# Turning g of two token units by DMA, and a rearranged tail, in an attention + two-layer-MoE kernel

## The chip, the cores and the metric

The kernel runs on one core of one Trainium2 chip. The metric is the device time of one execution in microseconds (us): 638.88 us, the median of three runs (637.43 to 639.08). The changed kernel is measured in the same way.

## What is computed (the reference, cut)

```python
# attention, batch 4, 8 heads, 576 tokens, head size 64
scores = q @ k.T / 8;  keep scores >= rowmax - tau;  a = softmax(kept) @ v
x = a as (2304 tokens, 512)
# first layer: w_in (512, 2048), w_out (2048, 512)
g = relu(x @ w_in) ** 2
x = g @ w_out
# second layer: phi (512, 32 slots), 8 experts of 4 slots, w1 (512, 1024), w2 (1024, 512) each
logits = x @ phi
slot_input = softmax_over_tokens(logits).T @ x
slot_out[e] = relu(slot_input[e] @ w1[e]) @ w2[e]
out = softmax_over_slots(logits) @ slot_out
```

## The kernel before, in words

**Stages.** While attention is computed, w_in is split into two fp16 parts (the `w8` tiles), w_out is rounded, stored to DRAM as `w_out32`, and multiplied with phi into `wphi`, so that the logits come straight from g. The 2304 tokens are taken as nine units of 256: eight of them (batch, half), and `rem` for the 64 last tokens of each batch. The units run in the order n = 0 to 8.

**A unit** (`ffn_ops`). DVE makes two fp16 parts of x: `xh` (line 1131) and `xl` (line 1136; there is one `xl` buffer, so a unit's `xl` waits for the last matmul of the unit before). PE makes eight pairs of column blocks `f_a`, `f_b` (line 1165), each half 8 matmuls with `xh` and 4 with `xl`. ACT applies relu and square (lines 1174, 1182) and leaves g in a `gt` tile of 128 columns x 2 x 256 tokens.

**What follows a unit** (`post`), put into the stream after the next unit's first pair: PE multiplies g with `wphi` (`pl`, line 977), turns the logits (lines 984, 990), and DVE and ACT make maxima, exponentials and token weights. Then g itself is needed with tokens on the partitions: for each of two token blocks t and four j, PE turns four 128x128 blocks (`turn`, line 269), ACT moves them from PSUM to `gk` (line 1074), PE multiplies with the token weights (`accum`, line 1089), and DVE adds to `sg` (line 1098). There are four `gk` buffers.

**The order of work.** All instructions are written by a planner (`Plan`): each operation has an engine, a cost, a key, and the slots it takes; the planner runs them in its own clock and writes each engine's stream in that order. Engines then execute their own stream in order, and SP issues all DMAs, loads of weights and transposes of attention alike, in one stream. `LEAD` shifts the keys. After the last attention operation (`plan.run(att)`) attention's memory is given back and nine 1 MiB loads `ew8` and one 0.5 MiB load `ew6` of expert weights are issued directly, outside the planner's clock and bus; then the planner goes on with the rest, loads into `xp` and `w8` slots (`w_load`) among them.

**The tail.** `sg` is turned and multiplied with w_out (line 1283; w_out lies in eight `raw64` tiles), then w1 (`hidden`, line 1302) and w2 (line 1376) of the eight experts, then the outputs (lines 1395 to 1414). 33.6 MB of w1 and w2 stream in; the loads `wr` go into the `raw64` slots once line 1283 has used them, and further `ew8` loads follow once w1 tiles are used. The loads, the planner's loop around the direct loads:

```python
plan.run(att)
...
for f in [ew8] * 9 + [ew6]:
    f()
for n in range(XPB + 1):
    add("w_load", "SP", 0.5, wx, state["xl"][-XPB - 1 + n], n, dma=1.46)
```

Of the kernel before, what the change touches and what calls it, by code (L numbers as in the profile page):

```python
# [147 lines left out]
def tile_kernel(  # L148
# [51 lines left out]
    LEAD = {'c_evac': 8.5, 'c_hi': 109.5, 'c_lo': 76.5, 'c_load': -19.6, 'c_low': 0.2, 'c_out': -17.5, 'c_prod': 65.3, 'c_scale': 13.2, 'c_shift': -19.8, 'c_store': -158.3, 'c_unit': 0.1, 'f_a': 18.2, 'f_acc': 7.3, 'f_alpha': -43.9, 'f_b': -30.4, 'f_cmax': -2.3, 'f_csum': -1.6, 'f_dk': 3.5, 'f_l4': -7.7, 'f_max': 43.7, 'f_merge': 5.1, 'f_p12': -4.1, 'f_pl': 278.3, 'f_pm': -7.7, 'f_relu': 3.3, 'xhi': 3.4, 'xlo': -1.1, 'f_gk': 15.9, 'w_load': 17.8, 'c_turn': 0.0, 'f_sq': -4.5, 'f_p1k': 2.2, 'lphi': -16.2, 'f_turn': 1.5, 'f_p3': -14.5, 'recip': 2.7, 'dturn': -3.1, 'q_scale': -2.9, 'p_evac': -20.3, 'f_total': 0.3, 'w_rest': -1.1, 'av': -1.0, 'r_evac': -3.3, 'w_hi': 6.6, 'w_scale': 0.3, 'v_hi': -6.8, 'top': 3.1, 'eps': -10.6, 'w_diag': -4.8, 'low': -4.3, 'v_scale': -9.2}  # L200
# [3 lines left out]
    GKD = ()  # L204
# [9 lines left out]
    QL = 19.2  # L214
# [86 lines left out]
    def conv_ops():  # L301
# [168 lines left out]
        for n in range(RB):  # L470
            add("w_pre", "SP", 0.5, lambda: state["wr"](), stores, 1000.0 + n, ["raw64"], dma=1.46)
# [485 lines left out]
    def ffn_ops(units):  # L957
# [9 lines left out]
        def post(u, d, first, last):  # L967
            w, po = {}, {}
            fo = prev["ops"]

# [42 lines left out]
            def cmax():  # L1013
                lk = w["p12"][:, NU:NU + T * NS].rearrange("p (t s) -> p t s", s=NS)
# [40 lines left out]
            add("f_csum", "DVE", 0.80, csum, [h], HI + 1, rel=[("mm", b_)])  # L1055
            i_ = add("f_p3", "PE", 0.25, p3, [e], pk(), ["mm"], [("dT", e)])
            j_ = add("f_dk", "DVE", 0.2, dkc, [i_], HI, rel=[("mm", i_)])
            lastsg, turns = fo.get("sg"), []
            for t in range(T):
                gks, ro = [], []  # L1060
                for j in range(NG):
# [54 lines left out]
        for n, u in enumerate(units):  # L1116
# [80 lines left out]
            pending = lambda u=u, d=d, n=n: post(u, d, n == 0, n == len(units) - 1)  # L1197
# [282 lines left out]
```

## Time and profile before

| what | value |
|---|---|
| median of 3 runs | 638.88 us |
| the profiled execution | 640.07 us, its span 638.3 us |
| PE busy | 585.2 us (92%) |
| ACT, DVE, POOL busy | 442.0, 432.4, 284.0 us |
| DMA engines busy (hardware queue) | 67.1% of the span, 115.88 MB |
| attention's last operation, by line 894 | ends at 483.6 us |
| units 7 and 8 | 498.8 to 529.7 and 529.7 to 560.7 us |
| w1 and w2 by PE | 579.3 to 619.7 us |

Times in the rows are us from the span's start; the execution's own time is 1.8 us more than its span. A busy PE counts pipelined matmuls, so PE is best read by the starts of its groups. `PEclk` is the granted TensorE clock, 1.00 being 2.4 GHz and 0.50 being 1.2 GHz.

### The profile page before, as it was taken

The numbers are of one execution on the slowest core, as the hardware profiler recorded it, in microseconds if no ns is written. First come the engines' busy times: TensorE is split into PE (matmuls) and PEld (weight loads), VectorE is DVE, ScalarE is ACT, GpSimd is POOL, SyncE is SP. The second block draws the span as 40 slices with busy tenths as digits, with TensorE's granted clock in tenths as the row PEclk, the third lists the DMA queues.
The fourth block names the chain that finished last, engine by engine and source line by source line (L and its number), as shares of the span: only waits on it lengthen the run. The fifth ranks groups of instructions, "written<-read, shape, count | busy, mean of one in ns | idle before, by whom it ended". The sixth has DMA issues, their size and how long they took to land.

```text
span 638.3 us, 14121 instructions
## 1 busy us (share of the span) xinstructions
PE 585.2 (92%) x5218; PEld 406.2 (64%) x5218; DVE 432.4 (68%) x1225; ACT 442.0 (69%) x852; POOL 284.0 (44%) x464
## 2 busy tenths in 40 slices
PE   3897979899999999999999989999999999989883
PEld 1454646567777677667767767867868787853321
DVE  5798998899988987986888987887640302021503
ACT  2798757678888888988978888887864545441203
POOL 1446672257577766676746657765530000010000
PEclk9998889989999999999989999999999999998997
DMA  8975516576887767585855857788646921568967
GB/s 277 351 232 170 193 58 222 183 184 162 206 152 165 175 137 138 102 197 97 183 106 98 179 103 140 133 174 166 149 75 240 407 80 34 185 213 315 388 253 296
DMA packets 156084, 116.78 MB, mean 183 GB/s; under 512 B 119920, under 2 KB 128880, under 8 KB 156016
## 3 DMA queue, kind: packets, MB, share of 16 engines
q1 hardware_dynamic: 156016, 115.88, 67.1%
q8 instruction: 41, 0.67, 0.4%
q14 instruction: 27, 0.22, 0.1%
HBM read 73.72 MB, written 8.91 MB: 129 GB/s over the span
## 4 chain that ended last, share of the span: by engine, by line
PE 66%; DVE 15%; DMA 6%; ACT 4%; issue 3%; POOL 3%; SPq 2%; ACTq 0%; DVEq 0%; POOLq 0%
PE mm L1165 28%; PE mm L269 8%; PE s L703 6%; PE po L872 5%; DVE u L729 5%; DVE e L745 3%; PE mm L1302 2%; PE mm L1089 2%; DMA w<-in_moe_w_dram 2%; PE mm L977 2%; PE s L690 2%; DMA w_out<-cv 2%; PE po L877 2%; PE po L864 1%; DMA qt<-in_q_dram 1%
## 5 line engine op out<-in xcount | busy, mean ns | idle before, releaser
L1165 PEld LDWEIGHTS <-w 128*128 128x128 f16 x1728 | 166.5, 98 | 26.8 <-issue 7.9
L768 POOL TENSOR_TENSOR hl<-e,hl 128x288 f16<-128x288 f32 x192 | 147.0, 789 | 40.1 <-issue 28.5
L1165 PE MATMUL mm<-xh,w 128*128 128x256 f16 x1152 | 149.6, 273 | 0.3 <-ACT gk L1074 0.2
L745 DVE SCALAR_TENSOR_TENSOR e<-u,sm,e 128x576 f32<-128x576 f32 x144 | 120.1, 849 | 18.7 <-ACT e L741 14.3
L741 ACT ACTIVATE e<-u,sm 128x576 f32<-128x576 f32 x144 | 109.2, 771 | 20.6 <-DVE u L729 15.3
L735 POOL TENSOR_SCALAR sm<-sm,tau_p 128x1 f32<-128x1 f32 x144 | 72.8, 511 | 72.0 <-DVE u L729 65.4
L1165 PE MATMUL mm<-xl,w 128*128 128x256 f16 x576 | 86.4, 273 | 0.0
L1174 ACT ACTIVATE gt<-mm,scl 128x512 f32<-128x512 f32 x72 | 49.2, 683 | 53.5 <-PE mm L1165 52.9
L729 DVE TENSOR_SCALAR_CACHE_REDUCE u<-s,raw 128x576 f32<-128x576 f32 x90 | 71.1, 811 | 14.7 <-PE s L703 13.7
L764 ACT ACTIVATE hl<-e 128x576 f16<-128x576 f32 x96 | 64.0, 675 | 2.0 <-DVE e L745 1.6
L832 POOL TENSOR_SCALAR sm<-sm 128x4 f32<-128x4 f32 (+1 forms) x48 | 20.8, 433 | 61.6 <-DVE e L745 52.1
L1182 ACT ACTIVATE gt<-gt 128x512 f32<-128x512 f32 x72 | 45.0, 625 | 1.1
L1265 POOL MEMSET cv<- 128x512 f32 x4 | 1.9, 524 | 97.4 <-PE mm L1089 97.4
L729 DVE TENSOR_SCALAR_CACHE_REDUCE u<-s,nscale 128x576 f32<-128x576 f32 x54 | 42.6, 807 | 3.2 <-PE s L690 2.6
L812 ACT ACTIVATE pt<-mm 128x512 f32<-128x512 f32 x48 | 28.6, 602 | 21.3 <-PE mm L269 20.8
L1074 ACT ACTIVATE gk<-mm 128x512 f32<-128x512 f32 x68 | 36.2, 591 | 6.3 <-PE mm L269 6.1
L269 PE MATMUL mm<-ident_r,e 128*128 128x128 f32 (+1 forms) x224 | 37.1, 300 | 3.1 <-DVE e L745 2.2
L703 PEld LDWEIGHTS <-qt 128*128 128x128 f16 (+3 forms) x400 | 21.9, 99 | 28.3 <-issue 17.8
L269 PE MATMUL mm<-ident_r,gt 128*128 128x128 f32 x288 | 38.0, 278 | 0.5 <-ACT gk L1074 0.5
L269 PEld LDWEIGHTS mm<-ident_r,e 128*128 128x128 f32 (+1 forms) x224 | 27.9, 153 | 16.3 <-DVE e L745 5.5
L872 PE MATMUL po<-pt,vh 128*64 128x256 f16 x576 | 37.0, 279 | 0.0
L269 PEld LDWEIGHTS mm<-ident_r,gt 128*128 128x128 f32 x288 | 31.8, 144 | 7.9 <-issue 5.8
(189 smaller groups left out, 978.2 us busy)
## 6 DMA issues: line engine op xcount, KB each, us to landing
w<-in_moe_w_dram SPq DMA_DIRECT2D x17, 1024.0 KB, 14.2
w<-in_moe_w_dram SPq DMA_DIRECT2D x26, 512.0 KB, 7.9
raw<-in_moe_w_in_dram SPq DMA_DIRECT2D x16, 511.8 KB, 6.7
raw<-in_moe_w_out_dram SPq DMA_DIRECT2D x16, 511.8 KB, 3.9
raw<-in_v_dram SPq DMA_DIRECT2D x20, 256.0 KB, 3.3
w_out<-cv SPq DMA_DIRECT2D x16, 256.0 KB, 2.7
w<-w_out SPq DMA_DIRECT2D x8, 512.0 KB, 4.2
kt<-in_k_dram SPq DMA_DIRECT2D x10, 320.0 KB, 3.5
```

Source lines behind the costliest of these rows:

```text
L269: nc.tensor.transpose(out_, in_, ident[:n, :n])
L703: nc.tensor.matmul(o0, d["qh"][r, a, q0], kk, start=full, stop=not full)
L729: nc.vector.tensor_scalar(u, o["s"][:, s0:s0 + S], d.get("nscale", nscale), None, ALU.mult, ALU.min, accum_out=gd["sm"][:, c:c + 1])
L735: nc.gpsimd.tensor_scalar(sm[:, 4 + c:5 + c], sm[:, c:c + 1], tau_p, None, ALU.add)
L741: nc.scalar.activation(e, o["u", a], AF.Exp, scale=-1.0, bias=gd["sm"][:, c:c + 1])
L745: nc.vector.scalar_tensor_tensor(e, o["u", a], sm[:, 4 + c:5 + c], e, ALU.is_le, ALU.mult, accum_out=sm[:, 8 + c:9 + c])
L764: nc.scalar.activation(o["hl"][:, a * S:(a + 1) * S], o["e"][:, a * S:(a + 1) * S], AF.Copy)
L768: nc.gpsimd.tensor_tensor(o["hl"][:, 2 * S:][:, i], o["e"][:, i], o["hl"][:, i], ALU.subtract)
L872: nc.tensor.matmul(po[64 * a:64 * a + 64, :n_], d["vh"][:, y, c0:c0 + D], gd["pt"][:, :, c + 5 * a + m, :], start=i == 0 and m == 0, stop= ...
L1165: nc.tensor.matmul(o["h"][:, i * NU:(i + 1) * NU], a, c, start=n_ == 0, stop=n_ == len(terms) - 1)
L1174: nc.scalar.activation(g, o["h"], AF.Relu, scale=down)
L1182: nc.scalar.activation(g, g, AF.Square)
```

## The change

For the units n = 6 and 7 (`DTU`), the 32 PE transposes of g and the ACT moves behind them are replaced. ACT (`f_part`) copies each pair's g, seen as 16-bit words, into high and low halves in a `raw64` tile; one DMA transpose (`f_move`, on SP) turns such a tile of two pairs, 16 blocks of 128x128; DVE (`f_join`) puts the two halves together again into `gk`. In the units 0 to 5 half of the `gk` moves go from ACT to DVE (`GKD`), in the last unit too. The eight loads of w_out into `raw64` get a later key. In the tail, both halves of w1 are multiplied together, w1 and w2 tiles hold consecutive rows of four (a partition reads up to 8 KB in one run, where w1 had runs of 4 KB and w2 of 2 KB), PSUM tiles alternate between the two pools of four banks (`bank`), and a few copies in the chain from `sg` to the slots are split or joined. Many `LEAD` values differ. The core of the diff:

```diff
...
     FKEY = 1e5
-    GKD = ()
+    DTU = (6, 7)
+    DEA = (0, 1)
+    GKL = (1, 3)
+    GKD = (1, 3)
     SQD = ()
     LOD = (0, 4)
...
     def mm_tile(tag="mm"):
         return psp[tag].tile([128, 512], F32, tag=tag, name="mm")
+
+    def old_tile():
+        return psp["old"].tile([128, 512], F32, tag="mm", name="mm")
...
+    def row512x2():
+        return rows.tile([128, 4 * CW], U16, tag="raw64", name="raw64", bufs=RB)
...
-            add("w_pre", "SP", 0.5, lambda: state["wr"](), stores, 1000.0 + n, ["raw64"], dma=1.46)
+            add("w_pre", "SP", 0.5, lambda n=n: state["wr"](state["wo"][n]), stores, 2 * FKEY + n, ["raw64"], dma=1.46)
...
-        def post(u, d, first, last):
+        def post(u, d, first, last, by_halves):
...
             def p1k():
-                p = w["p12"]
+                p = w["p1"] = old_tile() if last else w["p12"]
...
-            add("f_csum", "DVE", 0.80, csum, [h], HI + 1, rel=[("mm", b_)])
             i_ = add("f_p3", "PE", 0.25, p3, [e], pk(), ["mm"], [("dT", e)])
             j_ = add("f_dk", "DVE", 0.2, dkc, [i_], HI, rel=[("mm", i_)])
+            add("f_csum", "DVE", 0.80, csum, [h] + [j_] * last, HI + 1, rel=[] if last else [("mm", b_)])
...
+            halves = {}
+            for j in range(NG) if by_halves else ():
+                o = {}
+
+                def part(x, j=j, o=o):
+                    if not x:
+                        o["h"] = row512x2().rearrange("p (h x n) -> p h x n", h=2, x=2)
+                    g = d["pair"][2 * j + x].bitcast(U16).rearrange("p (n h) -> p h n", h=2)
+                    if x in DEA:
+                        nc.scalar.activation(o["h"][:, :, x], g, AF.Copy)
+                    else:
+                        nc.vector.tensor_copy(o["h"][:, :, x], g)
+
+                def move(j=j, o=o):
+                    o["t"] = row512x2().rearrange("p (b f) -> p b f", f=128)
+                    nc.sync.dma_start_transpose(out=o["t"], in_=o["h"].rearrange("p h x n -> p (h x n)"))
+
+                hs = []
+                for x in range(2):
+                    eng = "ACT" if x in DEA else "DVE"
+                    hs.append(add("f_part", eng, 1.05 if x in DEA else 1.13, lambda x=x, f=part: f(x), [d["sq"][2 * j + x]] + hs[:1],
+                                  pk(), [] if x else ["raw64"]))
+                    plan.release(hs[x], [("gt", d["rl"][2 * j + x])])
+                    plan.release(a, [("gt", d["rl"][2 * j + x])])
+                halves[j] = o, add("f_move", "SP", 3.0, move, hs, pk(), ["raw64"], [("raw64", hs[0])], dma=-4.5)
...
-                        if j not in GKD:
+                        if j not in gkd:
...
+                    if by_halves:
+                        def join(t=t, j=j):
+                            gk = w["gk", t, j] = row512()
+                            y = gk.bitcast(U16).rearrange("p (m f h) -> p h m f", m=4, h=2)
+                            z = halves[j][0]["t"].rearrange("p (h m t) f -> p t h m f", h=2, t=T)[:, t]
+                            for h in range(2):
+                                nc.vector.tensor_copy(y[:, h], z[:, h])
+
+                        rel = [("raw64", halves[j][1])] if t == T - 1 else []
+                        r = add("f_join", "DVE", 1.2, join, [halves[j][1]], pk(), ["gk"], rel)
+                        gks.append(("gk", r))
+                        ro.append(r)
+                        continue
...
+                    d.setdefault("pair", {})[m2] = g
...
-            pending = lambda u=u, d=d, n=n: post(u, d, n == 0, n == len(units) - 1)
+            pending = lambda u=u, d=d, n=n: post(u, d, n == 0, n == len(units) - 1, n in DTU)
...
-        src = {k: x.rearrange("(k p) f -> p k f", p=128) for k, x in src.items()}
...
+        def part(kind, e, k0, n):
+            x = src[kind, e]
+            if kind == "wo":
+                return x.rearrange("(k p) f -> p k f", p=128)[:, k0:k0 + n]
+            return x.rearrange("(h p k) f -> p h k f", p=128, k=4)[:, k0 // 4, k0 % 4:k0 % 4 + n]
...
         for kind, n in (("wo", 2), ("w1", E), ("w2", E)):
-            seq += [(kind, e, k) for e in range(n) for k in range(src[kind, e].shape[1])]
+            if kind == "w1":
+                seq += [(kind, e, k + i) for b in range(0, E, NG) for k in (0, 2) for e in range(b, b + NG) for i in range(2)]
+            else:
+                seq += [(kind, e, k) for e in range(n) for k in range(rows_of[kind])]
...
-            nc.sync.dma_start(out=t, in_=src[kind, e][:, k0:k0 + n, :])
+            nc.sync.dma_start(out=t, in_=part(kind, e, k0, n))
...
-        pt = mm_tile()
+        turns = [0]
+
+        def bank():
+            turns[0] += 1
+            return old_tile() if turns[0] % 2 else mm_tile()
+
+        pt = [bank() for _ in range(2)]
         for i in range(4):
-            transpose(pt[:, i * 128:(i + 1) * 128], sg[:, i * 128:(i + 1) * 128])
+            transpose(pt[i // 2][:, i % 2 * 128:(i % 2 + 1) * 128], sg[:, i * 128:(i + 1) * 128])
...
-        both(sgt, pt)
+        nc.scalar.activation(sgt[:, 0:256], pt[0][:, 0:256], AF.Copy)
+        nc.vector.tensor_copy(sgt[:, 256:512], pt[1][:, 0:256])
...
-        both(si4, ps, rr)
...
+        nc.scalar.activation(si4, ps, AF.Copy, scale=rr)
...
-        def hidden(i2, hf):
-            ph = mm_tile()
-            for kk in range(KC):
-                for j in range(NG):
...
+        def hidden(i2, kks, ph):
+            for kk in kks:
+                for hf in range(2):
+                    for j in range(NG):
...
+        def relu(ph):
+            hr = [row512() for _ in range(2)]
+            nc.scalar.activation(hr[0], ph[0], AF.Relu)
+            nc.vector.tensor_scalar(hr[1], ph[1], 0.0, None, ALU.max)
             return hr
...
-        h00 = hidden(0, 0)
-        c0 = spaced(0)
-        h01 = hidden(0, 1)
-        spread(0, 0, h00)
-        codes(*c0)
-        for _ in range(7):
+        ph = [bank() for _ in range(2)]
+        hidden(0, (0, 1), ph)
+        for _ in range(3):
             ew8()
...
+        codes(*pc[0])
+        ew8()
+        hidden(0, (2, 3), ph)
+        h0 = relu(ph)
+        for _ in range(3):
+            ew8()
+        c2 = codes_turn(*spaced(8))
+        ph = [bank() for _ in range(2)]
+        hidden(1, (0, 1), ph)
+        codes(*pc[1])
+        for hf in range(2):
+            spread(0, hf, h0[hf])
         for f in [ew8] + [wx] * 4 + [w8]:
             f()
-        c3 = spaced(12)
-        spread(1, 1, h11)
-        c4 = spaced(16)
-        codes(*c3)
-        codes(*c4)
-        po = mm_tile()
+        hidden(1, (2, 3), ph)
+        h1 = relu(ph)
+        codes(*c2)
+        c3, c4 = [codes_turn(*spaced(t)) for t in (12, 16)]
+        po = bank()
...
         for i, (e, fc) in enumerate(seq):
+            if i == NG:
+                for hf in range(2):
+                    spread(1, hf, h1[hf])
+                codes(*c3)
+                codes(*c4)
...
+            state["wo"] = [take(1024) for _ in range(RB)]
...
             plan.run(att)
+        psp["old"] = psp["mm"]
         psp["mm"] = ctx.enter_context(tc.tile_pool(name="ps_t", bufs=4, space=bass.MemoryType.PSUM))
...
```

What the planner makes of it is shown at two places. The first is SP's stream after the last attention transposes (`pt<-hl`): `w<-in_moe_w_dram` are loads of w1 and w2, `w<-w_out` loads of w_out. Before:

```order
L775 DMA_TRANSPOSE pt<-hl 128x18x128 x4
L1220 DMA w<-in_moe_w_dram 128x2x1024 x9
L1220 DMA w<-in_moe_w_dram 128x2x512
L1220 DMA w<-in_moe_w_dram 128x1024 x12
L1220 DMA w<-in_moe_w_dram 128x512 x8
L1220 DMA w<-in_moe_w_dram 128x1024 x2
L1220 DMA w<-in_moe_w_dram 128x2x512 x6
L1220 DMA w<-in_moe_w_dram 128x4x512 x8
```

With the change (`raw<-raw` are the new transposes, four of unit 6 and four of unit 7; 128x2048 is a 1 MiB load, 128x1024 one of 0.5 MiB):

```order
L784 DMA_TRANSPOSE pt<-hl 128x18x128 x7
L1279 DMA w<-in_moe_w_dram 128x2048 x9
L1279 DMA w<-in_moe_w_dram 128x1024 x3
L1084 DMA_TRANSPOSE raw_7191<-raw_7054 128x16x128
L1084 DMA_TRANSPOSE raw_7252<-raw_7189 128x16x128
L1084 DMA_TRANSPOSE raw_7316<-raw_7250 128x16x128
L1279 DMA w<-in_moe_w_dram 128x1024
L1084 DMA_TRANSPOSE raw_7380<-raw_7314 128x16x128
L1084 DMA_TRANSPOSE raw_7549<-raw_7412 128x16x128
L1084 DMA_TRANSPOSE raw_7616<-raw_7506 128x16x128
L1084 DMA_TRANSPOSE raw_7670<-raw_7582 128x16x128
L1279 DMA w<-in_moe_w_dram 128x1024
```

The new transposes stand behind the twelve loads that begin when attention ends, and one more 0.5 MiB load stands ahead of each unit's fourth transpose; the loads of w_out come after them all.

The second place is DVE's stream between the last attention operation (`xp<-po`, line 894 before, 903 now) and the column maximum `nm` of unit 6. Before (`xl<-xp` is unit 7's):

```order
L894 SCALAR_TENSOR_TENSOR xp<-po,mx,rr 128x256
L1131 TENSOR_SCALAR xh<-xp,scl 128x256
L1136 SCALAR_TENSOR_TENSOR xl<-xp,scl,xh 128x256
L1131 TENSOR_SCALAR xh<-xr,scl 128x256
L1136 SCALAR_TENSOR_TENSOR xl<-xp,scl,xh 128x256 x3
L1131 TENSOR_SCALAR xh<-xr,scl 128x256 x3
L994 TENSOR_REDUCE nm<-mm 32x1
```

With the change (`gk<-raw_7191` is the `f_join` of unit 6's first transpose, `gk<-raw_7252` that of its second):

```order
L903 SCALAR_TENSOR_TENSOR xp<-po,mx,rr 128x256
L1179 TENSOR_SCALAR xh<-xp,scl 128x256
L1119 COPY gk<-raw_7191 128x512 x2
L1184 SCALAR_TENSOR_TENSOR xl<-xp,scl,xh 128x256
L1179 TENSOR_SCALAR xh<-xr,scl 128x256
L1184 SCALAR_TENSOR_TENSOR xl<-xp,scl,xh 128x256 x3
L1179 TENSOR_SCALAR xh<-xr,scl 128x256
L1119 COPY gk<-raw_7252 128x512 x2
L1179 TENSOR_SCALAR xh<-xr,scl 128x256 x2
L1004 TENSOR_REDUCE nm<-mm 32x1
```

The first join stands ahead of all four `xl` of unit 7, the second ahead of unit 6's maximum. PE's stream has 64 transposes of `gt` fewer (288 before, 224 now); the first matmuls of unit 7 follow directly on unit 6's `pl`.

## Rows read from the trace of the kernel before

**Rows 1.** The chain of waits in order of time: start, us, engine, tile, line, count.
```profile
560.77 2.07 PE mm L977 x31
...
573.07 3.76 PE mm L1283 x32
...
606.85 11.73 DMA w<-in_moe_w_dram
```

**Rows 2.** Windows of PE: stretch, its length, PE busy (x instructions), PEclk, DMA share, GB/s.
```profile
150.00:483.00 333.00, 326.23 (x3279) 0.99 0.70 142
483.00:577.00 94.00, 91.09 (x837) 1.00 0.54 199
```

**Rows 3.** A group by line: the PE transposes of `gt`; busy us, mean ns.
```profile
L269 PE MATMUL mm<-ident_r,gt 128*128 128x128 f32 x288 | 38.0, 278 | 0.5 <-ACT gk L1074 0.5
```

**Rows 4.** Timeline of PE, unit 7 with unit 6's post: start, us, engine, line, operation.
```profile
498.75 2.13 PE L977 MATMUL mm<-gt,wphi 128*32 128x256 f32 x32
...
503.76 1.04 PE L1165 MATMUL mm<-xh,w 128*128 128x256 f16 x8
...
529.72 2.14 PE L977 MATMUL mm<-gt,wphi 128*32 128x256 f32 x32
```

**Rows 5.** Loads `w` on SP: the first after attention, then the twelfth (ns, start; landing).
```profile
DMA to landing us min/median/max: 5.0/5.0/5.0
...
L1220 SPq DMA_DIRECT2D w<-in_moe_w_dram x1: 3617/3617/3617, 497.8 to 497.8; - x1
...
DMA to landing us min/median/max: 16.7/16.7/16.7
```

**Rows 6.** DMA transposes: one alone; one behind two loads (452.4), one behind that.
```profile
DMA to landing us min/median/max: 4.6/4.6/4.6
...
L775 SPq DMA_TRANSPOSE pt<-hl x2: 2824/3406/3988, 452.4 to 456.5; - x2
...
DMA to landing us min/median/max: 4.7/5.6/6.5
```

**Rows 7.** Timeline of DVE around the end of attention and of unit 6's matmuls.
```profile
483.14 0.48 DVE L894 SCALAR_TENSOR_TENSOR xp<-po,mx,rr 128x256 f32<-128x256 f32 x1 [3.82 <-PE po L877]
...
498.86 0.48 DVE L1136 SCALAR_TENSOR_TENSOR xl<-xp,scl,xh 128x256 f16<-128x256 f32 x1 [14.85 <-PE mm L1165]
...
499.53 1.27 DVE L1136 SCALAR_TENSOR_TENSOR xl<-xp,scl,xh 128x256 f16<-128x256 f32 x3
```

**Rows 8.** Groups by line, DVE copies of 512 elements: busy us, mean ns | idle.
```profile
L329 DVE CAST raw<-raw 128x512 f16<-128x512 bf16 x16 | 14.5, 954 | 0.0
...
L1330 DVE COPY gk<-ctok 128x512 f32<-128x512 f32 (+1 forms) x5 | 2.0, 396 | 0.1
```

**Rows 9.** Windows of PE after two gaps; PEclk is the fourth column.
```profile
60.00:68.00 8.00, 6.83 (x22) 0.57 0.30 114
579.00:583.00 4.00, 3.71 (x20) 0.57 0.95 346
```

**Rows 10.** Windows of SP's DMA, loads of 4 KB runs, then of 2 KB: PEclk, share, GB/s.
```profile
486.00:510.00 24.00, 1.00 1.03 409
605.00:615.00 10.00, 1.00 1.05 387
```

**Rows 11.** Waits of PE from 483 to 579: us in total, times, longest.
```profile
PE mm L269 <- DVE rs L1270: 0.9, 1, 0.9
...
PE mm L269 <- ACT dT L1000: 0.4, 1, 0.4
```

**Rows 12.** Groups by line, ACT copies: shapes, busy us, mean ns.
```profile
L1174 ACT ACTIVATE gt<-mm,scl 128x512 f32<-128x512 f32 x72 | 49.2, 683 | 53.5 <-PE mm L1165 52.9
...
L1182 ACT ACTIVATE gt<-gt 128x512 f32<-128x512 f32 x72 | 45.0, 625 | 1.1
...
L331 ACT ACTIVATE raw<-raw 128x512 f16<-128x512 bf16 x16 | 21.7, 1375 | 11.0 <-DMA raw<-in_moe_w_in_dram 10.4 <-DMA raw<-in_moe_w_out_dram 0.6
...
L550 ACT ACTIVATE vh<-raw 128x512 bf16<-128x512 f32 x16 | 10.0, 623 | 1.3 <-DMA raw<-in_v_dram 1.3
```

More of the change, by code (lines that the diff above doesn't have):

```diff
@@ L213, in tile_kernel @@
     XHA = ()
-    QL = 19.2
+    QL = 18.24
     LL = 16.0
@@ L965, in ffn_ops @@
         HI = -1e5
-        def post(u, d, first, last):
+        def post(u, d, first, last, by_halves):
             w, po = {}, {}
             fo = prev["ops"]
+            gkd = GKL if last else GKD
             def pl(lo, hi):
@@ L1225, in take @@
             kind, e, _ = seq[0]
-            n = width // src[kind, e].shape[2]
+            n = width // src[kind, e].shape[1]
             rs = [r for r in seq[:n] if r[:2] == (kind, e)]
+            assert kind == "wo" or rs[0][2] // 4 == rs[-1][2] // 4
             del seq[:len(rs)]
@@ L1262, in tail, with spaced, codes_turn, codes @@
             wg()
+        NTL = B * S // 128
+        ct = {}
+        def spaced(t0):
+            w = min(4, NTL - t0)
+            cd = row512().rearrange("p (t g s) -> p t g s", t=4, g=NG)
+            nc.vector.tensor_copy(
+                cd[:, :w], ctok[:, t0:t0 + w, :].unsqueeze(2).to_broadcast([128, w, NG, NS])
+            )
+            return t0, w, cd
+        def codes_turn(t0, w, cd):
+            pt = bank()
+            for t in range(w):
+                transpose(pt[:, t * 128:(t + 1) * 128], cd[:, t].rearrange("p g s -> p (g s)"))
+            return t0, w, pt
+        def codes(t0, w, pt):
+            if t0 == 0:
+                ct["a"] = state["ew"].tile([128, 2048], F32R, tag="ew8", name="cts", bufs=9)
+                ct["b"] = fx.tile([128, 512], F32R, tag="xl", name="cts", bufs=1)
+            dst = ct["a"][:, t0 * 128:(t0 + w) * 128] if t0 < 16 else ct["b"][:, 0:w * 128]
+            src = pt[:, :w * 128]
+            nc.scalar.activation(dst, src, AF.Copy)
+            for r in (32, 96):
+                nc.vector.tensor_tensor(dst[r:r + 32], src[r:r + 32], dst[r:r + 32].bitcast(F32), ALU.subtract)
         hz = [[row512(F32, "cv", CB).rearrange("p (j c s) -> p j c s", j=NG, c=4) for _ in range(2)] for _ in range(2)]
@@ L1278, in tail @@
         nc.vector.tensor_copy(rr, p0[:, 0:1])
-        ps = mm_tile()
+        cs = [spaced(4 * t) for t in range(2)]
+        ps = bank()
         for i in range(4):
@@ L1288, in tail @@
         si4 = row512()
-        both(si4, ps, rr)
-        pq = mm_tile()
+        nc.scalar.activation(si4, ps, AF.Copy, scale=rr)
+        pc = [codes_turn(*c) for c in cs]
+        pq = bank()
         for kk in range(KC):
             nc.tensor.matmul(
-                pq[:, kk * NS:(kk + 1) * NS], si4[:, kk * 128:(kk + 1) * 128], stack_i, start=True, stop=True
+                pq[:, kk * NS:(kk + 1) * NS], si4[:, kk:DM:4], stack_i, start=True, stop=True
             )
@@ L1296, in tail @@
         nc.vector.tensor_copy(sit.rearrange("p a b -> p (a b)"), pq[:, :KC * NS])
[L1298 to L1310 removed]
+        def hidden(i2, kks, ph):
+            for kk in kks:
+                for hf in range(2):
+                    for j in range(NG):
+                        nc.tensor.matmul(
+                            ph[hf][NS * j:NS * j + NS, :],
+                            sit[:, kk, :],
+                            W["w1", NG * i2 + j, kk][:, hf * 512:(hf + 1) * 512],
+                            start=kk == 0,
+                            stop=kk == KC - 1,
+                        )
+        def relu(ph):
+            hr = [row512() for _ in range(2)]
+            nc.scalar.activation(hr[0], ph[0], AF.Relu)
+            nc.vector.tensor_scalar(hr[1], ph[1], 0.0, None, ALU.max)
             return hr
         def spread(i2, hf, hr):
[L1314 removed]
+            pt = bank()
             for c in range(4):
[L1316 removed]
+                transpose(pt[:, c * 128:(c + 1) * 128], hr[:, c:512:4])
             for j in range(NG):
@@ L1384, in tail @@
         both(so4, po)
-        pr = [mm_tile() for _ in range(2)]
+        pr = [bank() for _ in range(2)]
         for i in range(2):
```

53 lines of the change are left out of this document (7 added, 46 removed).

## The prediction

> **What bounds the kernel now.** I read the chain of waits first, then PE's windows and its timeline, then what SP and DVE do when attention ends. PE is the bound up to the tail: it is idle for 6.8 of 333 us during attention and for 2.9 of the 94 us after it [rows 2]. Units 7 and 8 follow each other at PE's own pace: unit 6's `pl` starts at 498.75 and unit 7's at 529.72, 30.97 us later [rows 4]. In the tail the bound changes. Line 1283 ends at 573.07 + 3.76 = 576.8, and from then on the chain ends in a load of w2 that lands at 606.85 + 11.73 = 618.6 [rows 1]. So an end of the loads needs two things: the `raw64` slots that line 1283 gives back, and the DMA's rate. A microsecond saved on PE before line 1283 is a microsecond off the end, as long as what line 1283 waits for is there.
>
> **What the change removes.** The PE transposes of `gt` cost 38.0 / 288 = 0.132 us each [rows 3], and the order of PE's stream shows 64 fewer. That is 8.4 us, all on the bound: **-8.4**.
>
> **What it adds, and what stands in front of it.** The new path of g is ACT copy, DMA transpose, DVE join. In itself it has room: PE needs the joined g only after several further pairs of the next unit. But two streams decide when it runs.
>
> SP's stream has the twelve loads that begin when attention ends, then unit 6's first transpose. In the trace these loads queue up: the first lands 5.0 us after its issue, the twelfth, issued at 497.85, only 16.7 us after it, at 514.6 [rows 5]. They are 11.0 MB, and at 409 GB/s [rows 10] that is 27 us of a full DMA. A transpose behind loads waits too: one alone lands after 4.6 us, one issued at 452.4 behind two loads after 6.5 us; the next, issued at 456.5, lands 4.7 us later, 2.3 us after the one before it [rows 6]. In the changed stream PE has done half a pair less (1.3 us) when attention ends, so I move this 1.3 us forward: loads down at 513.2, unit 6's first transpose at 513.2 + 2.3 = **515.5**.
>
> DVE's stream has the join of that very transpose ahead of unit 7's four `xl`. In the trace these run from 498.86, when unit 6's last matmul frees their buffer, to 499.53 + 1.27 = 500.80 [rows 7], which is when PE has finished `pl` (498.75 + 2.07 = 500.8 [rows 1, 4]). With the change they wait until 515.5 plus a join. A join is two copies of 512 16-bit words to steps of 4 bytes, which the trace does not have. Whole words of 512 take 0.40 us, 16-bit ones at steps of 8 bytes with a change of type 0.95 [rows 8]; that bounds a join by 0.8 and 1.9, and I take the middle, 1.4, since its steps are half as long. So the `xl` end at 515.5 + 1.4 + 1.94 = 518.8, 18.0 us later than now. PE can use 1.0 us of that for its eight `xh` matmuls [rows 4]. **+17.0**, with bounds of 16.4 and 17.5 from the join.
>
> After such a gap PE runs slower. In 60 to 68, after an idle stretch, the granted clock is 0.57 on average, mostly its 1.2 GHz level, a loss of 8 x 0.43 = 3.4 us; in 579 to 583, after short gaps, 4 x 0.43 = 1.7 [rows 9]. The new gap is long, but what follows is dense fp16 work, which I cannot place; I take the middle: **+2.5**.
>
> **What is hidden, and by what.** Unit 6's other transposes land at some 2.3 us each behind the first, the fourth behind a load that waits for unit 7's `xl`; unit 6's weights times g come four pairs later. Unit 7's transposes are issued as its g appears, its last one behind a load that waits for unit 8's `xl`, and are needed five pairs into unit 8, over 10 us later. The joins have DVE almost alone (idle for 14.85 us before `xl` now [rows 7]). ACT gets eight copies of 1024 16-bit words per unit and loses eight moves; twice the 0.62 of 512 words would be 1.25 each, and with relu 0.68 and square 0.63 a unit's eight pairs cost 20.5 us [rows 12], less than the 26.8 that PE is left with (30.97 - 4.2). Cost: nothing, and if the copies are dearer, the rival below. The eight w_out loads (4.2 MB) now come after unit 7, between loads into `w8` slots; behind unit 8's last matmul there remain some 2.6 MB, 6.4 us, while PE needs 573.07 - 560.77 = 12.3 us to line 1283 [rows 1]. Nothing, with some 4 us of cover.
>
> **Attention** loses the w_out loads and sends 24 of its ACT moves to DVE. PE is busy 98% there, so between a gain of the whole idle 6.8 us and a loss of a few I take nothing, and 3 us either way for the range.
>
> **The tail.** The chain from `pl` to line 1283 has one long wait of PE, 0.9 for DVE's reciprocal, which stays, and 0.4 for ACT's exponentials [rows 11], behind moves that now are shared with DVE: **-0.4**, bounds 0 and -1.3. Behind line 1283 15.2 MB remain, nearly all w2. Its runs of 2 KB go at 387 GB/s, w1's of 4 KB at 409 [rows 10]; with runs of 4 and 8 KB I take 409: 39.3 - 37.2 = **-2.1**, bounds 0 and -3. The Trainium skill ("DMA: Bandwidth & Descriptors", section "Why small descriptors are slow (HBM only)") gives each packet about 3 cycles beside its 32-byte beats; by that, 2 KB costs 67 cycles for 64 and 8 KB 259 for 256, 3.4% instead of the row's 5.4%, an estimate of -1.3 here and a sum 0.8 us higher. The rows decide. The last 19.7 us, outputs, are not touched but for PSUM banks that nothing waits for.
>
> **The sum:** -8.4 + 17.0 + 2.5 - 0.4 - 2.1 = +8.6. Against the profiled execution, 640.07, that is 648.7; the median of the runs is 1.2 lower, 638.88, and gives **647.5 us**. Its own range, with attention's 3 us, the clock's 0.9 and the bounds of the tail, is 642 to 653.
>
> **Rivals.**
> *The transposes pass the loads* (ends on the other side). SP still issues them after the twelfth load, whose issue ends at 497.85 + 3.62 = 501.5 [rows 5], 500.2 with the shift; alone they would land 4.6 us later, at 504.8, and the `xl` end at 508.1: a delay of 6.3 instead of 17.0, with the smaller loss of clock 1.7. Sum -8.4 + 6.3 + 1.7 - 0.4 - 2.1 = -2.9, 636.0 us, and as low as 629 if attention's idle time went too. It decides whether the first transpose lands before about 507. Against it: 6.5 after loads, 4.6 alone. Chance 0.12.
> *Attention gives it back*: its idle 6.8 us go, since the reordered ACT and DVE work frees PE; 640.7 us, no change. For it: ACT is relieved; against: nothing in 98% says which wait it would end. Chance 0.06.
> *ACT becomes the bound*: a strided 16-bit copy of 512 words on ACT takes 1.37 now [rows 12]. If the new copies go at that price, 2.75 each, a unit needs 8 x 4.06 = 32.5 us of ACT against PE's 26.8, 5.7 us more in unit 7, unit 6's share being lost in the gap: 653.2 us. Against it: only the read side has steps here. Chance 0.06.
> That the change does not remove the transposes is excluded by PE's order.
>
> **How the numbers follow.** The forecast keeps 0.76. A difference under 0.3%, 1.9 us, cannot be told from none. Faster: the first rival, and a sliver of the forecast with every bound low, 0.13; same: the second and the edge of the others, 0.07; slower 0.80. 636 to 654 takes in the forecast's range, the second rival, the first at its upper edge and the third: 8 in 10.
>
> **What would show it.** Right: in the new trace PE idles for some 17 us just after unit 6's `pl`, waiting for DVE's `xl`, DVE itself for a DMA transpose into `raw`, landing about 31 us after the twelve loads began; then a clock near 0.5 for a few us; unit 8's `pl` near 572 instead of 560.7; w2 loads above 400 GB/s. Wrong: unit 7's `xl` ending near 501, or a landing long before the loads are down; then the sum turns to a gain. A gap spread over many relu waits would show the third rival.

## The result and the profile after

The changed kernel takes 645.25 us (median of six runs, 642.58 to 649.82), the kernel before beside it 637.83 (637.29 to 639.08). The ratio is 1.0122, with a 95% interval of 1.0077 to 1.0168: 1.2% slower, clear of no change. The profiled execution took 643.08 us, span 641.3.

The chain of waits after (start, us, what), which answers to [rows 1]:

```profile
479.62 17.02 PE mm L1213 x156
496.64 15.96 DMA raw<-raw
512.62 0.79 DVE gk L1119 x2
513.41 0.36 DVE xl L1184
...
515.28 2.93 PE mm L1213 x13
...
578.57 3.64 PE mm L1379 x32
```

A DMA transpose of g (`raw<-raw`), a join (line 1119) and an `xl` (line 1184) now stand on the chain. DVE's timeline, against [rows 7], shows the same stretch:

```profile
512.62 0.79 DVE L1119 COPY gk<-raw 128x512 uint16<-128x512 uint16 x2 [32.09 <-DMA raw<-raw]
513.30 0.48 DVE L1184 SCALAR_TENSOR_TENSOR xl<-xp,scl,xh 128x256 f16<-128x256 f32 x1
513.69 0.35 DVE L1179 TENSOR_SCALAR xh<-xr,scl 128x256 f16<-128x256 f32 x1
513.96 1.27 DVE L1184 SCALAR_TENSOR_TENSOR xl<-xp,scl,xh 128x256 f16<-128x256 f32 x3
```

PE's timeline, against [rows 4]; `pl` is line 987 now, the matmuls line 1213:

```profile
496.58 2.13 PE L987 MATMUL mm<-gt,wphi 128*32 128x256 f32 x32
498.65 1.05 PE L1213 MATMUL mm<-xh,w 128*128 128x256 f16 x8
513.83 0.37 PE L1213 MATMUL mm<-xl,w 128*128 128x256 f16 x1 [14.13 <-DVE xl L1184]
514.49 1.16 PE L1213 MATMUL mm<-xl,w 128*128 128x256 f16 x3 [0.29 <-DVE xl L1184]
...
540.75 2.14 PE L987 MATMUL mm<-gt,wphi 128*32 128x256 f32 x32
...
567.52 1.91 PE L987 MATMUL mm<-gt,wphi 128*32 128x256 f32 x32
```

Windows of all engines (PE, PEld, DVE, ACT, POOL busy, PEclk, DMA share, GB/s), against [rows 2, 9, 10]:

```profile
503.00:514.00 11.00, 0.17 (x1) 0.10 (x1) 1.38 (x5) 0.00 (x0) 0.00 (x0) 0.50 1.12 279
514.00:519.00 5.00, 4.66 (x18) 2.11 (x16) 2.69 (x9) 0.72 (x2) 0.00 (x0) 0.50 1.08 226
519.00:530.00 11.00, 11.00 (x98) 8.77 (x98) 4.27 (x17) 8.95 (x15) 0.00 (x0) 1.00 0.51 97
...
592.00:608.00 16.00, 11.92 (x102) 4.63 (x95) 6.04 (x17) 3.00 (x6) 0.00 (x0) 1.00 1.02 422
```

So the two profiled executions differ like this, by the starts of `pl` and of line 1379 (1283 before):

| stretch | before | after | difference |
|---|---|---|---|
| start to unit 6's `pl` | 498.75 | 496.58 | -2.2 |
| to unit 7's `pl` | 30.97 | 44.17 | +13.2 |
| to unit 8's `pl` | 30.98 | 26.77 | -4.2 |
| to line 1379 | 12.37 | 11.05 | -1.3 |
| to the end of the span | 65.2 | 62.7 | -2.5 |
| span | 638.3 | 641.3 | +3.0 |

All of the loss is the one stretch with the gap. The +3.0 understates it: this execution is 2.2 us shorter than its kernel's median and the one profiled before 2.2 us longer than its own (640.07 against 637.83), which makes up the difference to the medians' +7.4.

### The profile page after: what moved, and what is told of

Read it like the earlier page. It is cut to its first block, busy times and chain, and to the rows that moved or that the text cites. A ratio compares the mean times of both kernels' runs of the same rounds, so it can differ in the third digit from the quotient of the medians.

```text
span 641.3 us, 14020 instructions
## 1 busy us (share of the span) xinstructions
PE 571.6 (89%) x5154; PEld 398.5 (62%) x5154; DVE 456.3 (71%) x1286; ACT 436.9 (68%) x822; POOL 282.2 (44%) x464
## 4 chain that ended last, share of the span: by engine, by line
PE 63%; DVE 16%; issue 6%; DMA 5%; POOL 4%; ACT 4%; SPq 1%; DVEq 0%; POOLq 0%; ACTq 0%
PE mm L1213 27%; PE mm L275 7%; PE s L712 6%; PE po L881 4%; DVE u L738 4%; DVE e L754 3%; PE mm L1137 3%; DMA raw<-raw 2%; PE mm L1399 2%; PE mm L987 2%; PE po L873 2%; PE s L699 1%; DMA qt<-in_q_dram 1%; PE po L886 1%; POOL hl L777 1%
## 5 line engine op out<-in xcount | busy, mean ns | idle before, releaser
L777 POOL TENSOR_TENSOR hl<-e,hl 128x288 f16<-128x288 f32 x192 | 151.1, 814 | 45.0 <-issue 35.6
L754 DVE SCALAR_TENSOR_TENSOR e<-u,sm,e 128x576 f32<-128x576 f32 x144 | 121.4, 861 | 8.8 <-ACT e L750 4.1
L1213 PE MATMUL mm<-xl,w 128*128 128x256 f16 x576 | 87.7, 274 | 14.5 <-DVE xl L1184 14.4
L744 POOL TENSOR_SCALAR sm<-sm,tau_p 128x1 f32<-128x1 f32 x144 | 68.9, 485 | 70.4 <-DVE u L738 58.1
L1119 DVE COPY gk<-raw 128x512 uint16<-128x512 uint16 x32 | 11.9, 447 | 32.1 <-DMA raw<-raw 32.1
L712 PE MATMUL s<-kt,qt 128*128 128x512 f16 (+1 forms) x200 | 32.9, 289 | 1.8 <-DVE u L738 1.7
L881 PEld LDWEIGHTS <-vh 128*64 128x64 f16 x576 | 29.6, 110 | 6.9 <-issue 6.6
## 6 DMA issues: line engine op xcount, KB each, us to landing
w<-in_moe_w_dram SPq DMA_DIRECT2D x26, 512.0 KB, 6.6
w<-w_out SPq DMA_DIRECT2D x8, 512.0 KB, 6.4
```

What stands on the lines that cost most here:

```text
L712: nc.tensor.matmul(o0, d["qh"][r, a, q0], kk, start=full, stop=not full)
L744: nc.gpsimd.tensor_scalar(sm[:, 4 + c:5 + c], sm[:, c:c + 1], tau_p, None, ALU.add)
L754: nc.vector.scalar_tensor_tensor(e, o["u", a], sm[:, 4 + c:5 + c], e, ALU.is_le, ALU.mult, accum_out=sm[:, 8 + c:9 + c])
L777: nc.gpsimd.tensor_tensor(o["hl"][:, 2 * S:][:, i], o["e"][:, i], o["hl"][:, i], ALU.subtract)
L881: nc.tensor.matmul(po[64 * a:64 * a + 64, :n_], d["vh"][:, y, c0:c0 + D], gd["pt"][:, :, c + 5 * a + m, :], start=i == 0 and m == 0, stop= ...
L1213: nc.tensor.matmul(o["h"][:, i * NU:(i + 1) * NU], a, c, start=n_ == 0, stop=n_ == len(terms) - 1)
```

## The experiments

Ratios are to the kernel before, measured beside each (its medians there: 638.38 us for runs 1 to 4, 638.12 for 5 to 8, 638.61 for 9 to 12). A and B are the theories that each expectation sets against each other. The gap is PE's idle stretch before unit 7's first `xl` matmul.

**1. Joins behind `xl`.**

```diff
-                        r = add("f_join", "DVE", 1.2, join, [halves[j][1]], pk(), ["gk"], rel)
+                        r = add("f_join", "DVE", 1.2, join, [halves[j][1], *after], pk(), ["gk"], rel)
```

`after` holds the next unit's four `xl`.

> Edit: the joins of a unit are placed behind the next unit's four xl in DVE's stream; the DMA transposes stay behind the twelve loads in SP's stream. Theory A (the landing of the transposes is the cause, DVE's order only passes it on to the next unit's first matmuls): PE's idle 14.1 us before unit 7's first xl matmul goes, but PE now comes to unit 6's weights times g (line 1137) at about 511, 11.5 us of full-clock work later, and the fourth transpose lands near 512.6 + 3 x 2.3 = 519.5; so a gap of about 9 us appears there, and some 5 us are gained: about 640 us against the 645 of the changed kernel, ratio to the kernel before about 1.004. Theory B (DVE's order is the whole cause, g is needed late enough): no gap, 14.1 us and the 2.4 us of low clock are gained, about 629, ratio 0.986. Theory C (the transposes' landing has nothing to do with it, and PE waits for something else): 645 and the same gap.

Measured: 646.5 us (644.12 to 651.63), 1.0138 [1.0093, 1.0183]; nothing gained. DVE's and PE's timelines:

```profile
518.42 0.79 DVE L1119 COPY gk<-raw 128x512 uint16<-128x512 uint16 x2 [1.60 <-DMA raw<-raw]
519.36 0.41 DVE L1004 TENSOR_REDUCE nm<-mm 32x1 f32<-32x256 f32 x1
```
```profile
520.66 0.42 PE L275 MATMUL mm<-ident_r,dT 32*128 32x32 f32 x2 [12.22 <-ACT dT L1010]
```

The gap moved, as A has it, but not to line 1137: the joins now stood ahead of DVE's maximum of the logits (line 1004), whose exponentials PE needs some 8 us after `xl`. So this run does not free PE of DVE's order and does not by itself exclude B. The times do, by an estimate: PE stopped at 508.4 and had 5.6 us of full-clock work to line 1137, so it would be there at 514, while the last of the four joins that it needs there ran only at 526.0. A still later place of the joins would have moved the gap again, not removed it.

**2 and 4. Fewer loads ahead of the first transpose.** In the second, `f_dk` also waits for the merge of the unit before, since there is one `dk` buffer.

```diff
-        for f in [ew8] * 9 + [ew6]:
+        for f in [ew8] * 4:
             f()
+        for n, f in enumerate([lambda r=take(2048): ew8(r) for _ in range(5)] + [ew6]):
+            add("e_load", "SP", 0.5, f, [state["moves"][0]], 2 * FKEY - 100 + n, dma=2.56 if n < 5 else 1.46)
```

`state["moves"][0]` is unit 6's first `f_move`; the fourth run has `()` there, and its planner put two of the five large loads ahead of it.

> Edit: four of the nine large direct loads and two small ones stay ahead of unit 6's first DMA transpose in SP's stream (5.2 MB instead of 11.0 MB); the others follow it. Theory A (the transpose waits for the bytes ahead of it, at 409 GB/s): it lands 5.8 MB / 409 GB/s = 14.1 us sooner, near 498.5 instead of 512.6, unit 7's xl end near 501, PE's gap shrinks from 14.1 to at most 2 us and the low clock behind it goes; 14 to 16.5 us are gained: 629 to 631 us, ratio to the kernel before 0.986 to 0.990, and the runs lie within 2 us of each other if the spread of the changed kernel's runs (642.6 to 649.8) comes from the clock after the gap. Theory B (the transposes are slow whatever stands ahead, or share the DMA with loads issued behind them): landing after 506 and a gap of 6 us or more, 637 us or more. Theory C (the loads bind the end, so a faster PE only waits in the tail): the gap goes, but the time stays above 640.

> Edit: as the second kernel of this set, but six large and two small loads stay ahead of unit 6's first transpose (7.3 MB instead of 11.0 MB). Theory A: the landing comes 3.7 MB / 409 GB/s = 9.0 us sooner, near 503.6; PE's gap shrinks from 14.1 to about 5 us; 9 to 11 us are gained: 634 to 636 us. Theory B (the loads ahead do not set the landing): landing and gap unchanged within 2 us, 643 or more.

Measured: the second 634.75 us (630.83 to 639.05), 0.9944 [0.9916, 0.9972]; the fourth 643.69 (635.82 to 644.95), 1.0063 [1.0031, 1.0095]. The join and the first `xl` matmul by DVE's and PE's timelines, of the second (its lines stand one further down), then of the fourth:

```profile
499.67 0.79 DVE L1120 COPY gk<-raw 128x512 uint16<-128x512 uint16 x2 [18.69 <-DMA raw<-raw]
```
```profile
500.88 0.27 PE L1214 MATMUL mm<-xl,w 128*128 128x256 f16 x1 [0.74 <-DVE xl L1185]
```
```profile
507.58 0.79 DVE L1119 COPY gk<-raw 128x512 uint16<-128x512 uint16 x2 [25.48 <-DMA raw<-raw]
```
```profile
508.79 0.37 PE L1213 MATMUL mm<-xl,w 128*128 128x256 f16 x1 [7.52 <-DVE xl L1184]
```

From the first load's issue (480.65, 481.78, 480.21) to the join the first transpose took 19.0, 25.8 and 32.4 us with 5.2, 7.3 and 11.0 MB ahead of it: 13.4 us for 5.8 MB, 430 GB/s. The landing and the gap follow the bytes, as A says. The times follow less well. The second profile gains 16.3 us up to unit 8's `pl` (551.25), but gives 5.9 back behind it (14.4 us to line 1380 where the changed kernel takes 11.05 to line 1379, then 65.2 to the end instead of 62.7), and its median is 4 us above A; the cause of that stays open. The runs are as spread as ever, so the clock after the gap cannot be the whole cause of the spread. The fourth's median gained 1.6 us of the 9 to 11, though its profiled gap is half as long. What the record shows of both is that an execution's time goes with its mean granted clock: in the fourth from 635.82 us at 0.978 to 644.95 at 0.961, in the second from 630.83 at 0.985 to 639.05 at 0.970. The fourth's profiled execution (640.11 at 0.969) is 3.6 us below its median; in which stretch the longer ones lose their clock, no trace shows.

**3 and 5. No unit turned by DMA; the changed tail alone.**

```diff
-DTU = (6, 7)
+DTU = ()      # fifth run: also GKD = (), LEAD, QL and w_pre's key as before
```

> Edit: no unit is turned by DMA; the changed tail, the shared moves on DVE and the place of the w_out loads stay. Theory A: no gap, the 64 PE transposes (8.4 us) are back, and against the kernel before only the tail's gain of 2 to 3 us and a part in attention of 0 to 2 us is left: 633 to 636 us, ratio 0.992 to 0.998, with runs within 2 us of each other. Theory B (the tail or the moved w_out loads cost time too, and the gap is not the whole loss): 639 or more.

> Edit: the kernel before with the changed tail alone: no unit turned by DMA, and the shares, keys and w_out loads of attention as before. Theory A (the changed tail gains the 2.5 us that the profiles show between line 1379 or 1283 and the end, less a drop of the clock or two; the third kernel's 641.3 is the changed order of attention): 635.5 to 638.5 us, ratio to the kernel before 0.995 to 1.000, PE without the idle stretches at 412 to 420 and 460 to 470 us, unit 6's pl at 498.7 as before. Theory B (the changed tail costs time, and the third kernel's loss is there): 640 or more.

Measured: 641.32 (637.8 to 644.94), 1.0049 [1.0023, 1.0076], and 635.4 (632.71 to 638.18), 0.9947 [0.9921, 0.9973]. The third came out as its B. The changed tail gains 2.7 us by the medians; what is left in the third, the new shares and lead times (those of the units' operations among them) and the later place of the w_out loads, costs 5.9. I call it the new order of attention. Two windows of the third, then of the changed kernel:

```profile
412.00:416.00 4.00, 2.96 (x33) 2.00 (x33) 3.93 (x12) 2.26 (x8) 2.83 (x4) 1.00 0.27 52
416.00:424.00 8.00, 7.93 (x44) 5.93 (x45) 6.16 (x20) 5.20 (x9) 3.37 (x6) 0.57 0.80 156
```
```profile
412.00:416.00 4.00, 3.09 (x39) 2.16 (x37) 3.49 (x15) 2.61 (x9) 2.45 (x6) 1.00 0.41 78
416.00:424.00 8.00, 7.55 (x71) 5.69 (x72) 7.33 (x18) 6.86 (x12) 4.56 (x6) 1.00 0.87 129
```

With the new order PE is idle for about 1 us here, in the changed kernel waiting for `dT`, in the third for DVE's `nm` and ACT's `pt`, and again for 2 to 3 us near 465; before it was busy throughout 400:425 and 455:480. After the idle stretch the granted clock fell to 0.57 in the third, and it did not in the changed kernel's profile. It fell at one or both places in runs 1, 3 and 4 and at neither in run 2.

In the third's profile unit 6's `pl` starts 7.3 us later than in the fifth's, by PE's timelines:

```profile
502.99 2.13 PE L987 MATMUL mm<-gt,wphi 128*32 128x256 f32 x32
```
```profile
495.65 2.13 PE L987 MATMUL mm<-gt,wphi 128*32 128x256 f32 x32
...
568.93 3.64 PE L1379 MATMUL mm<-w,gk 128*32 128x512 f32 x32
```

The fifth's expectation of 498.7 was missed by 3.1 us, although attention is as in the kernel before: one execution differs from another there, in these two by the granted clock among others (1.00 against 0.97 in 100:150 and in 300:350). So 3 us between two profiles before unit 6's `pl` say nothing of the code.

**6, 7 and 8. The second kernel with attention's old order, or half of it.**

```diff
-GKD = (1, 3)              # sixth and seventh run
+GKD = ()
-LEAD, QL = new, 18.24     # sixth and eighth run
+LEAD, QL = old, 19.2
```

`new` and `old` stand for the whole lists of lead times, of the changed kernel and of the one before.

> Edit: as the second kernel (unit 6's first DMA transpose behind four large and two small loads), with the shares and keys of attention as in the kernel before (all moves of g before the last unit on ACT, the old lead times). Theory A (the changed order of attention makes PE idle for 1 us near 415 and 2 us near 465, after which the granted clock fell to 0.57 for some 4 us in the profiles of three of five changed kernels, 1.7 us each, and that is also the spread of the runs): these stretches go, unit 6's pl starts near 498.7, the median falls from 634.75 to 629 to 631.5, ratio 0.986 to 0.990, and the runs lie within 3 us of each other. Theory B (the spread and the 4 us come from after attention, or from the chip): 634 to 636 with a spread of 6 us or more.

> Edit: as the second kernel, with only the shared moves undone (all moves of g before the last unit on ACT again; the new lead times stay). If the idle stretches of PE near 415 and 465 come from DVE's additional moves, they go here, and the time is as with the old attention, 629 to 632; if they come from the lead times, they stay, 634 to 636.

> Edit: as the second kernel, with only the lead times (and the fixed start QL) of the kernel before; the moves stay shared between ACT and DVE. If the idle stretches of PE near 415 and 465 come from the lead times, they go here, 629 to 632; if they come from DVE's additional moves, they stay, 634 to 636.

Measured: 629.91 (629.04 to 633.99), 0.9877 [0.9841, 0.9913]; 638.72, 1.0000 [0.9976, 1.0025]; 640.88, 1.0027 [1.0005, 1.0049]. The sixth beats both kernels. Its `pl` of units 6 to 8, by PE's timeline:

```profile
496.84 2.14 PE L987 MATMUL mm<-gt,wphi 128*32 128x256 f32 x32
...
523.60 1.91 PE L987 MATMUL mm<-gt,wphi 128*32 128x256 f32 x32
...
549.04 1.91 PE L987 MATMUL mm<-gt,wphi 128*32 128x256 f32 x32
```

No gap is left, and turning by DMA now gains 5.5 us over the tail alone (635.4), of the 8.4 that PE saves. Neither half helps alone: both cost more than the whole new order does, so shares and lead times belong together and my either-or was no question. A's time came true. Its account of the spread did not: six runs within 5 us, and the fifth kernel, with PE busy all through 400:425 and 455:480, also spreads over 5.5.

Nor is it shown that PE's two idle stretches are what the new order costs. The second kernel's PE is idle for 1.4 us in 400:425 and 2.3 in 455:480, the sixth's for 0.5 and 0.2, and yet the second's `pl` of unit 6 starts only 0.2 us later; its PE has 2.4 us less idle time in 250:400:

```profile
497.02 2.14 PE L987 MATMUL mm<-gt,wphi 128*32 128x256 f32 x32
```

The other 3.8 us between these two profiles lie 2.0 before unit 7's `pl`, where the second still waits 0.74 and 0.39 us for `xl`, and 1.8 behind line 1380. The eighth kernel has neither idle stretch (25.00 and 24.88 us busy of 25) and is slower than both; its PE is idle for 6.4 us of 250:300 instead.

**9. The changed kernel with attention's old order.** GKD, LEAD and QL as before.

> Edit: the changed kernel (g of units 6 and 7 turned by DMA behind the twelve loads, the changed tail), with the shares and keys of attention as in the kernel before. It gives what the DMA turning alone costs over the fifth kernel (635.4, the tail alone). Theory A (the parts add up: the gap of 14 us and its low clock against 4.2 us of PE work saved in each of two units; in the profile of the changed kernel unit 6's pl to unit 8's pl takes 70.9 us, against 62.0 before, and from there to line 1379 1.3 less): 635.4 + 7.7 = 643, or, taking the 4.8 us between the second and the sixth kernel off 645.25, 640.4; so 640 to 643. Theory B (the changed order of attention costs nothing where the gap follows, the loss is the gap's alone): 645 or more.

Measured: 645.0 (642.24 to 649.48), 1.0111 [1.0077, 1.0146]. Over the tail alone (635.4), turning by DMA as the change does it, with the later w_out loads, costs 9.6 us; the new order of attention costs 0.2 more. B: with the gap the order costs nothing, without it 4.8 (second against sixth) or 5.9 (third against fifth), by the medians. Why the two don't add stays open. The two profiles nearly balance as well (spans of 640.1 and 641.3): the ninth's gap is 11.45 us instead of 14.13, but behind line 1379 it takes 64.9 us instead of 62.7.

**10. The old rows of w1 and w2** in the fifth kernel.

```diff
-            return x.rearrange("(h p k) f -> p h k f", p=128, k=4)[:, k0 // 4, k0 % 4:k0 % 4 + n]
+            return x.rearrange("(k p) f -> p k f", p=128)[:, k0:k0 + n]
...
```

> Edit: as the fifth kernel (tail alone), with the old layout of the rows of w1 and w2 (rows 128 apart in a partition, runs of 4 and 2 KB). Theory A (w2's stream binds the tail, and its rate falls from some 415 to 387 GB/s over the 12 to 15 MB behind line 1379): 2 to 3 us more than the fifth kernel, 637.5 to 638.5, with PE waiting for a load of w2 by some 2 us at the end of line 1456 where it waits 0.21 us in the fifth. Theory B (PE binds the changed tail): within 0.7 us of 635.4.

Measured: 636.95 (635.21 to 639.35), 0.9973 [0.9947, 0.9998], 1.5 us more than the fifth by the medians. Windows and PE of the tenth, then of the fifth:

```profile
600.00:610.00 10.00, 10.00 (x94) 2.81 (x88) 1.72 (x4) 0.00 (x0) 0.00 (x0) 1.00 1.04 386
```
```profile
611.30 1.05 PE L1456 MATMUL mm<-w,cv 128*32 128x512 f32 x4 [0.30 <-DMA w<-in_moe_w_dram]
612.66 1.05 PE L1456 MATMUL mm<-w,cv 128*32 128x512 f32 x4 [0.31 <-DMA w<-in_moe_w_dram]
613.97 1.05 PE L1456 MATMUL mm<-w,cv 128*32 128x512 f32 x4 [0.26 <-DMA w<-in_moe_w_dram]
615.28 1.05 PE L1456 MATMUL mm<-w,cv 128*32 128x512 f32 x4 [0.25 <-DMA w<-in_moe_w_dram]
```
```profile
595.00:605.00 10.00, 7.34 (x69) 3.17 (x68) 5.76 (x17) 1.35 (x3) 0.00 (x0) 1.00 1.01 418
```
```profile
614.04 1.05 PE L1456 MATMUL mm<-w,cv 128*32 128x512 f32 x4 [0.21 <-DMA w<-in_moe_w_dram]
```

The rate is A's, 386 against 418 GB/s. The gain lies between A and B: in the tenth PE waits for loads in line 1456 four times, 1.1 us in all, in the fifth once, so that with the new rows PE nearly sets the pace. The 1.5 us is not shown to be the stream's alone: in the two profiles the span ends 64.8 and 64.7 us behind line 1379, and 1.1 of the 1.3 us between them lie before unit 6's `pl`, where the two kernels have the same work. The Trainium skill ("DMA: Bandwidth & Descriptors", "Why small descriptors are slow (HBM only)") gives a packet a fixed overhead of about 3 cycles beside its 32-byte beats; an estimate from that is 3.4% between runs of 2 and 8 KB, and the two windows differ by 8%.

**11. The transposes on ACT's queue.**

```diff
-                    nc.sync.dma_start_transpose(out=o["t"], in_=o["h"].rearrange("p h x n -> p (h x n)"))
+                    nc.scalar.dma_start_transpose(out=o["t"], in_=o["h"].rearrange("p h x n -> p (h x n)"))
```

The rest is the ninth kernel.

> Edit: as the ninth kernel, with the DMA transposes of g issued by ACT into its own queue instead of SP's; the twelve loads stay where they are. Theory A (the transposes wait because they stand behind the loads in SP's queue): the first lands some 5 to 10 us after its second half is copied, before 497, and PE's gap before unit 7's first xl goes; ACT pays the issues, some 2 us each; 630 to 636. Theory B (the loads already handed to the DMA engines hold up whatever comes later, on any queue): the first still lands past 508, ACT stands still in the issue, and the time is that of the ninth kernel or worse, 640 or more.

Measured: 653.77 (652.94 to 654.56), 1.0246 [1.0210, 1.0281]. ACT's and PE's timelines:

```profile
495.36 1.43 ACTq L1084 DMA_TRANSPOSE raw<-raw  x1
...
500.54 11.20 ACTq L1084 DMA_TRANSPOSE raw<-raw  x1
511.80 0.69 ACT L1223 ACTIVATE gt<-mm,scl 128x512 f32<-128x512 f32 x1 [10.20 <-issue]
```
```profile
513.20 1.07 PE L987 MATMUL mm<-gt,wphi 128*32 128x256 f32 x4 [11.43 <-ACT gt L1231]
```

The first transpose landed at 512.0, 32.8 us after the first load's issue, no sooner than from SP. ACT stood from 487.4 until it could issue at 495.36, and again at the second one. B: what holds a transpose up is not only its place in SP's queue; loads handed to the DMA before it do so from ACT's queue too. What let ACT issue only at 495.36 (the program's own waits for earlier DMAs, or the DMA) was not separated. The Trainium skill ("DMA: Bandwidth & Descriptors", "Queues, rings and completion order") has each DMA engine go round the queues that have work for it, one packet at a time. By that a transpose on a queue of its own should slip in between the loads; the 16.6 us from issue to landing here, against 4.7 for the median transpose, don't agree.

**12. The sixth with the joins behind `xl`.** The edit of run 1 in the sixth kernel.

> Edit: as the sixth kernel (first transpose behind four large loads, old attention), with the joins behind the next unit's xl in DVE's stream. Theory A (once the transposes land in time, DVE's order does not matter): 629.9 within 1 us. Theory B (the joins then hold up the maximum, line 1004, as they did in the first kernel): 1 to 4 us slower, PE waiting for ACT's dT in unit 7.

Measured: 630.63 (628.08 to 637.11), 0.9898 [0.9857, 0.9939]: as the sixth. Once the landing is early, moving the joins costs nothing that these runs can tell.

## Why the prediction was right, step by step

The median came out at 645.25 against 647.5, inside the range, and the mechanism is the one foretold. The sum of +8.6 was made for the profiled execution and came out at +3.0 there, +7.4 in the medians.

- *64 PE transposes, -8.4*: right. Unit 8's stretch, free of gaps, is 4.2 shorter, half of it.
- *The gap, +17.0*: right in place and cause, 14.1 + 0.3 = 14.4 in size. The first transpose landed 32.4 us after the loads began (the sum had 33.1, with the loads before starting at 483.69; the 31 in its last paragraph leaves out the transpose's own 2.3) and 16.0 after unit 6's `pl` instead of 16.7, which is 0.7. A join takes 0.79 us instead of 1.4, which is 0.6; and PE went on after the first `xl`, not the fourth, 1.4 sooner. I treated the four as one. The stated reason, a place in SP's stream, is too narrow: run 11 shows the same wait from another queue.
- *The clock, +2.5*: 4.66 us of work in 514 to 519 at a granted 0.50, so 2.3. Right, though the 2.5 was only the middle between two rows.
- *The chain to line 1379, -0.4*: -1.3, at its bound.
- *The tail, -2.1*: -2.5 in the profile and -2.7 in the medians of run 5, but the agreement is partly luck. The step's mechanism, w2's rate, gives at most 1.5 of it (run 10). In run 5's profile only 1.0 us is gained up to line 1379 and 0.5 behind it; the rest lies before unit 6's `pl`. Over eleven profiles with the changed tail the stretch behind line 1379 takes 62.7 to 65.2 us, against 65.2 before, and the changed kernel's is the shortest of them. In it PE waits for no load in line 1456. Where the rest of the median's gain comes from, and what the tail's other edits give, which I had at nothing, stays open.
- *Attention, 0 with 3 either way*: -2.2 in the profile, no more than kernels with the same attention differ by (495.65 in run 5, 496.78 in run 10, 498.75 before); +0.2 in the medians (run 9). The bound held, but I did not see that the new order costs 5 to 6 us by the medians as soon as the gap is gone (runs 2, 3, 5, 6). It leaves PE idle twice; that this is the cost is not shown (run 8).
- *The parts together*: by the medians, tail -2.7 (run 5), turning +9.6 (run 9), order +0.2. They add up to the whole by construction, each being taken from the one before, so that is no test. Against the forecast it is: the terms for the turning, -8.4 + 17.0 + 2.5 = +11.1, measured 9.6.
- *Rivals*: transposes that pass the loads: excluded by the 32 us, and by run 11 for ACT's queue too. Attention giving it back: no. ACT as the bound: its copies of 1024 words take 1.06 us (below), not 2.75.

A group by line of the changed kernel, which answers to [rows 12]:

```profile
L1078 ACT ACTIVATE raw<-gt x16: 1039/1057/1058, 476.8 to 542.2; 128x1024 uint16<-128x1024 uint16 x16
```

## What to carry to other kernels

Hand a small transfer that somebody waits for over before a burst of large loads. Here moving it to another queue did not help once the loads were handed over, while a shorter burst ahead of it did: count the bytes ahead. A planner that does not see loads issued outside its clock, as this one, puts the work that depends on the transfer too early in an in-order stream, and everything behind it pays. With the burst cut in two and attention's old order, this change is 1.2% faster instead of 1.2% slower. And where executions of one kernel spread over 5 to 9 us, take a difference of a few us from medians; one profile against another shows where, not how much.

## What the runs showed of the hardware that I had not expected

- A DMA transpose behind loads held its issuing engine: 13.97 us of SP's issue for the longest (2.31 median), 11.20 on ACT, whose work for PE then stood still (run 11). Group by line of the changed kernel:

```profile
L1084 SPq DMA_TRANSPOSE raw<-raw x8: 1721/2310/13966, 496.6 to 543.3; - x8
...
DMA to landing us min/median/max: 4.2/4.7/16.0
```

- While the last loads drained beside transposes, the DMA was full at 279 GB/s (503 to 514), against 422 where only loads ran (592 to 608).
- Much the same idle stretch of PE, 0.9 to 1.0 us near 414, was followed by a granted clock of 0.57 in one execution (run 3) and 1.00 in another (the changed kernel) of kernels with nearly the same attention; run 1, with the changed kernel's attention and the same 0.91 us, had 0.57 in 416 to 420.
- The executions of one kernel differ in their mean granted clock, and the longer ones have the lower: the changed kernel's go from 642.58 us at 0.976 to 649.25 at 0.961.
- The two copies of a join, 512 16-bit words each to steps of 4 bytes, took DVE 0.79 us together, what two copies of whole words take [rows 8].
